# Three blocks of a first matmul by seven products instead of eight, with the instruction list made anew

## The chip, the cores and the metric

The kernel runs on one core of a Trainium2 chip. The metric is device time in microseconds, as the median of three runs. The engines are named as the profile names them: PE is TensorE, PEld its weight loads, DVE is VectorE, ACT is ScalarE, POOL is GpSimd, and SP is SyncE, whose queue issues most of the DMAs here.

## The reference

Retention (attention without a softmax, with a decay that depends on distance), followed by a dense two-layer network with a tanh-approximated GELU:

```python
# q, k, v: (8, 8, 576, 64)   batch, heads, positions, head_dim
gamma = 1.0 - 2.0 ** (-5.0 - np.arange(H))
Dmat = np.where(rel >= 0, gamma[:, None, None] ** rel, 0.0)      # rel = i - j
ret = (q @ k.transpose(0, 1, 3, 2)) / sqrt(64) * Dmat
x = (ret @ v).transpose(0, 2, 1, 3).reshape(4608, 512)           # tokens x d_model
h = x @ w_in                                                     # 512 -> 2048,  "mm1"
g = 0.5 * h * (1 + tanh(sqrt(2 / pi) * (h + 0.044715 * h**3)))
out = g @ w_out                                                  # 2048 -> 512,  "mm2"
```

## The kernel before

**The work.** The 4608 tokens are cut in two ways. Attention goes by *units*: 8 batches of 5 units (four of 128 positions and a tail of 64), numbered 0 to 39; eight of these are taken in pairs ("wide" units) at the start. The network goes by *blocks* of 512 tokens, numbered 0 to 8.

A unit's q, k and v are loaded into a slot of `pages` (7 slots of three pages, `raws[u % NR]`), cast to f16 with the decay factors (steps `q`, `k`, `v`), transposed (`D` by DMA, `t`/`y` by TensorE), and multiplied (step `B u,w`: scores and state sums of unit u, output of unit w). The masked scores (`m`), state sums (`a`, `o`) and f16 states (`z`) follow. Step `x` copies a unit's output, already transposed, into `xT`, a ring of 2048 tokens; mm1 reads its moving operand from there.

**mm1.** For a block, 2048 hidden features are made in 16 tiles of 128 features x 512 tokens. A step `N t,fc,part` takes two features' tiles for 256 of the tokens: 8 matmuls of 256 columns into one PSUM bank (line 708). A step `F` is the gelu of that bank on ScalarE, PSUM to the f16 tile `gT` (line 716). `M` and `G` are the same with other cuts (512 or 128 columns). The pool `ps_h` has two banks for this.

**mm2.** Blocks 1 to 7 and half of block 8 already go by a scheme of seven products: a pair of 128-token chunks, the two halves of the features and the two halves of the output columns form a 2 x 2 block product, and seven products of sums (`H`: sums of gT on VectorE into `ssum`; `T`: sums of w_out into `tsum`, made once) take the place of eight. A step `W t,pr,i` is one product (8 matmuls of 256 columns, line 809), a step `V t,pr,i` copies or adds a piece of the two banks of `ps_o` into the result tile `ost` (lines 241 and 768). The rest of mm2 are plain steps `O` (line 734) and `P` (line 857), and `S` and `Q` store.

**The order.** Nothing is scheduled by a framework. `ORDER` is a written list of some 1200 steps; the kernel walks through it and issues each step's instructions, so the list fixes the order on every engine and on every queue. Each engine works through its own instructions in that order; waits between engines follow from the tiles. A step that waits holds up whatever stands behind it on its engine or queue. `K` are filler matmuls near the start.

Of the kernel before, what the change touches and what calls it, by code (L numbers as in the profile page):

```python
# [10 lines left out]
AF = mybir.ActivationFunctionType  # L11
ALU = mybir.AluOpType
F32 = mybir.dt.float32
# [4 lines left out]
Z,1,v Z,2,g L,0,0 L,0,2 q,0 L,0,1 k,0,a L,2,0 v,0,g g I,2,g I,1,g K,4 K,2 t,0,q,o K,4 K,2 X,0 a,0,1  # L18
y,0,q,a q,2 I,0,g Z,3,v t,0,k,h y,0,k,v I,3,g z,0,1,a L,2,1 a,1,1 k,2,g K,4 K,4 K,2 t,2,k,h o,1,1
Y,0,1 L,4,1 I,5,g Z,4,g m,0,1 t,2,q,o k,4,a K,4 Y,0,0 y,2,k,a y,2,q,a z,1,1,v m,0,0 K,4 R,0 t,4,k,o  # L20
Y,2,1 I,4,g L,2,2 c Z,0,g x,1 x,0 K,3 N,0,0,0 m,2,1 L,4,0 N,0,2,0 I,7,g y,4,k,v v,2,g L,5,0 F,0,0,0
I,6,g N,0,6,0 F,0,6,0 F,0,2,0 Z,5,v L,5,1 X,2 q,4 Y,2,0 K,1 t,4,q,o N,0,4,0 N,0,10,0 a,2,1 z,2,1,v
m,2,0 k,5,g F,0,4,0 N,0,8,0 J,1,g y,4,q,v a,3,1 q,5 L,5,2 F,0,10,0 R,2 J,0,g B,4,-1 z,3,1,v t,5,q,o
# [26 lines left out]
H,2,0,2,v N,3,6,0 F,3,4,0 H,2,0,4,v S,1,1 H,2,1,1,v L,23,2 L,21,0 D,19 L,24,1 L,24,0 W,2,0,6  # L50
z,16,1,g V,2,0,2,a v,17,v B,17,16 a,17,0 V,2,0,1,v z,17,0,g a,17,1 N,3,2,0 S,1,2 x,16 m,17 F,3,6,0
W,2,0,7 z,17,1,v B,18,17 x,17 L,20,0 H,2,1,3,v W,2,0,5 L,22,1 L,25,0 F,3,2,0 V,2,0,3,v m,18 a,18,0
L,21,2 N,3,14,0 z,18,0,a a,18,1 W,2,0,4 V,2,0,4,v F,3,14,0 V,2,0,5,v N,3,8,1 q,21 L,22,0 W,2,0,3
k,21,v H,2,1,2,v W,2,1,1 V,2,1,0,a F,3,8,1 B,19,18 V,2,0,6,v j,0,a N,3,4,1 W,2,1,2 W,2,1,6 V,2,1,2,a
N,3,0,1 W,2,1,7 F,3,4,1 F,3,0,1 V,2,1,1,v S,1,3 V,2,1,3,v S,2,0 L,26,0 L,19,2 q,22 q,20 N,3,14,1
D,20 H,2,1,4,v F,3,14,1 v,20,g z,18,1,v x,18 L,22,2 W,2,1,4 N,3,6,1 W,2,1,5 V,2,1,5,v F,3,6,1
N,3,12,0 D,21 W,3,0,1 V,3,0,0,a L,25,1 F,3,12,0 N,3,10,1 m,19 v,19,v L,23,1 B,20,19 V,2,1,4,v a,20,0
L,23,0 k,22,g N,3,12,1 L,29,0 L,27,0 H,3,0,1,v H,3,0,2,v W,3,0,2 F,3,12,1 F,3,10,1 W,2,1,3 k,24,g
m,20 N,3,2,1 V,3,0,2,a V,2,1,6,v v,21,g x,19 a,20,1 z,20,0,g N,4,0,0 F,3,2,1 H,3,0,4,v v,22,g
B,21,20 k,23,a N,4,6,0 D,22 F,4,0,0 W,3,0,6 q,24 k,25,v F,4,6,0 N,4,4,0 H,3,0,3,v V,3,0,1,v N,4,12,0  # L60
F,4,4,0 a,21,0 x,20 a,21,1 H,3,1,1,v v,23,v z,20,1,a o,21,1 m,21 W,3,0,5 W,3,0,7 z,21,0,a D,24
V,3,0,3,v S,2,1 F,4,12,0 N,4,2,0 B,22,21 F,4,2,0 q,23 V,3,0,4,v H,3,1,2,v x,21 W,3,0,4 q,25
V,3,0,5,v L,26,1 a,22,0 W,3,0,3 S,2,2 L,27,2 m,22 N,4,12,1 W,3,1,1 z,22,0,a D,23 L,24,2 F,4,12,1
V,3,0,6,v q,27 N,4,2,1 j,5,v L,26,2 N,4,0,1 F,4,2,1 a,22,1 z,21,1,g z,22,1,a L,25,2 B,23,22 L,28,0
V,3,1,0,a N,4,14,0 W,3,1,2 F,4,0,1 H,3,1,3,v N,4,4,1 W,3,1,6 F,4,14,0 V,3,1,1,v i,4,v S,2,3 F,4,4,1
m,23 x,22 V,3,1,2,a M,4,8 G,4,8 W,3,1,5 v,24,g L,28,1 v,25,g M,4,10 a,23,0 q,26 v,26,v G,4,10 L,27,1
N,4,14,1 W,3,1,7 a,23,1 V,3,1,3,v F,4,14,1 L,31,2 z,23,1,g M,4,9 z,23,0,a L,29,1 k,27,a B,24,23
H,3,1,4,v N,4,6,1 D,25 G,4,9 k,26,a L,29,2 M,4,11 x,23 L,28,2 W,3,1,4 F,4,6,1 V,3,1,4,v V,3,1,5,v
D,26 m,24 W,3,1,3 N,5,0,0 G,4,11 i,5,g V,3,1,6,v B,25,24 q,28 F,5,0,0 L,30,2 S,3,0 H,4,0,1,v W,4,0,1
k,28,v H,4,0,2,v x,24 S,3,3 V,4,0,0,a a,25,0 z,25,0,v N,5,2,0 W,4,0,2 F,5,2,0 m,25 N,5,6,0 D,27 D,28  # L70
a,25,1 B,26,25 N,5,14,0 H,4,0,4,v v,28,g S,3,1 L,30,0 v,27,v F,5,6,0 V,4,0,2,a N,5,8,0 x,25 F,5,14,0
W,4,0,6 H,4,0,3,v F,5,8,0 a,26,0 a,26,1 V,4,0,1,v v,29,g z,25,1,g L,32,0 N,5,10,0 z,26,0,v W,4,0,7
L,31,1 N,5,4,0 V,4,0,3,v H,4,1,1,v W,4,0,4 m,26 F,5,10,0 H,4,1,2,v B,27,26 x,26 W,4,0,5 L,32,2
V,4,0,5,v F,5,4,0 N,5,10,1 o,26,1 N,5,4,1 q,29 F,5,10,1 V,4,0,4,v m,27 W,4,1,1 V,4,1,0,a L,30,1
N,5,12,0 S,3,2 a,27,0 L,35,0 W,4,0,3 q,30 H,4,1,3,v V,4,0,6,v k,30,v H,4,1,4,v F,5,12,0 W,4,1,2
j,7,g W,4,1,6 F,5,4,1 z,26,1,a N,5,6,1 z,27,0,g k,29,g a,27,1 N,5,14,1 V,4,1,2,a H,5,0,1,v L,31,0
q,31 V,4,1,1,v L,36,2 D,30 W,4,1,7 V,4,1,3,v k,31,a B,28,27 F,5,6,1 F,5,14,1 a,28,0 W,4,1,5 S,4,1
H,5,0,2,v N,5,12,1 a,28,1 D,29 V,4,1,4,v z,28,0,a x,27 v,31,g z,28,1,v z,27,1,g N,5,0,1 F,5,12,1
W,4,1,4 L,34,0 N,5,8,1 L,33,1 F,5,8,1 m,28 F,5,0,1 B,29,28 m,29 v,30,g i,7,a V,4,1,5,v W,4,1,3
N,5,2,1 x,28 B,30,29 L,34,1 F,5,2,1 H,5,0,4,v x,29 a,30,0 V,4,1,6,v W,5,0,1 m,30 H,5,0,3,v V,5,0,0,a  # L80
H,5,1,3,v v,32,v a,30,1 S,4,0 N,6,0,0 z,30,0,g L,33,0 W,5,0,2 q,33 W,5,0,6 V,5,0,2,a N,6,12,0
V,5,0,1,v W,5,0,7 D,31 B,31,30 F,6,0,0 k,34,a L,34,2 x,30 q,32 V,5,0,3,v H,5,1,1,v W,5,0,5 M,6,8
L,36,0 q,34 a,31,0 L,32,1 k,33,v L,33,2 F,6,12,0 W,5,0,4 H,5,1,2,v G,6,8 N,6,2,0 i,6,a m,31
V,5,0,5,v F,6,2,0 M,6,9 q,35 W,5,1,1 G,6,9 M,6,4 G,6,4 L,35,1 V,5,0,4,v L,38,1 N,6,2,1 S,4,2 S,5,1
z,30,1,g k,32,v L,39,2 F,6,2,1 D,32 W,5,0,3 M,6,5 a,31,1 V,5,1,0,a z,31,0,a j,4,a G,6,5 W,5,1,2
V,5,0,6,v M,6,11 B,32,31 v,33,g o,31,1 V,5,1,2,a W,5,1,7 M,6,6 G,6,11 S,5,0 S,4,3 a,32,0 G,6,6 x,31
z,32,0,a D,33 W,5,1,6 m,32 v,34,g V,5,1,1,v M,6,7 M,6,10 a,32,1 z,31,1,v j,1,a V,5,1,3,v z,32,1,a
B,33,32 L,37,1 a,33,0 W,5,1,4 L,36,1 G,6,7 N,6,0,1 k,36,a G,6,10 k,35,g z,33,0,a F,6,0,1 L,37,0
a,33,1 V,5,1,5,v L,35,2 v,35,g W,5,1,5 x,32 H,6,0,3,v m,33 N,6,12,1 D,34 D,35 H,5,1,4,v N,6,14,0
F,6,12,1 F,6,14,0 v,36,g B,34,33 q,36 V,5,1,4,v H,6,0,1,v N,6,14,1 W,6,0,1 W,5,1,3 k,38,a H,6,0,2,v  # L90
x,33 F,6,14,1 V,5,1,6,v V,6,0,0,a L,38,0 m,34 z,33,1,g N,7,0,0 F,7,0,0 B,35,34 L,38,2 q,38 W,6,0,2
V,6,0,2,a N,7,10,0 W,6,0,6 H,6,0,4,v H,6,1,1,v F,7,10,0 a,35,0 q,37 N,7,8,0 L,39,1 F,7,8,0 x,34 m,35
V,6,0,1,v z,35,0,a D,36 S,5,3 W,6,0,7 a,35,1 V,6,0,3,v z,35,1,g N,7,6,0 H,6,1,2,v W,6,0,4 k,37,g
N,7,2,0 D,37 B,36,35 V,6,0,5,v L,39,0 F,7,6,0 F,7,2,0 q,39 W,6,1,1 N,7,4,0 W,6,0,5 x,35 N,7,4,1
F,7,4,0 V,6,0,4,v L,37,2 W,6,0,3 N,7,0,1 F,7,4,1 S,5,2 i,3,a a,36,0 V,6,0,6,v a,36,1 N,7,2,1
V,6,1,0,a W,6,1,6 m,36 H,7,0,3,v v,38,v F,7,0,1 N,7,6,1 z,36,0,g V,6,1,1,v F,7,2,1 k,39,v W,6,1,2
N,7,12,0 F,7,6,1 V,6,1,2,a H,6,1,4,v D,39 v,37,g B,37,36 H,6,1,3,v W,6,1,5 W,6,1,7 x,36 N,7,14,0
o,36,1 z,36,1,a S,6,1 F,7,12,0 D,38 N,7,8,1 F,7,14,0 a,37,0 V,6,1,3,v V,6,1,4,v W,6,1,4 N,7,10,1
F,7,8,1 V,6,1,5,v W,7,0,1 a,37,1 m,37 W,6,1,3 z,37,0,v F,7,10,1 z,37,1,a S,6,0 N,7,12,1 B,38,37
i,2,g x,37 V,7,0,0,a F,7,12,1 j,2,v V,6,1,6,v H,7,0,1,v v,39,g N,7,14,1 F,7,14,1 H,7,0,2,v W,7,0,6  # L100
N,8,0,0 a,38,0 W,7,0,2 a,38,1 N,8,12,0 H,7,0,4,v F,8,0,0 m,38 H,7,1,1,v V,7,0,1,v S,6,3 N,8,2,0
z,38,0,v V,7,0,2,a W,7,0,7 S,6,2 F,8,2,0 F,8,12,0 W,7,0,5 B,39,38 V,7,0,3,v N,8,10,0 W,7,0,4 N,8,4,0
F,8,10,0 H,7,1,2,v V,7,0,4,v V,7,0,5,v x,38 W,7,1,1 W,7,0,3 V,7,1,0,a m,39 N,8,14,0 z,38,1,g B,-1,39
W,7,1,2 F,8,4,0 V,7,1,2,a N,8,6,0 V,7,0,6,v H,7,1,3,v F,8,14,0 W,7,1,6 N,8,8,0 W,7,1,7 H,7,1,4,v
x,39 F,8,6,0 V,7,1,1,v W,7,1,5 V,7,1,3,v W,7,1,4 F,8,8,0 N,8,10,1 N,8,14,1 V,7,1,5,v V,7,1,4,v
F,8,10,1 W,7,1,3 H,8,0,1,v W,8,0,1 V,8,0,0,a H,8,0,2,v N,8,0,1 S,7,3 F,8,14,1 F,8,0,1 V,7,1,6,v
S,7,2 W,8,0,6 V,8,0,1,v N,8,8,1 W,8,0,2 S,7,0 V,8,0,2,a S,7,1 H,8,0,3,v F,8,8,1 N,8,2,1 W,8,0,7
N,8,6,1 H,8,0,4,v W,8,0,5 F,8,2,1 V,8,0,3,v F,8,6,1 W,8,0,4 N,8,12,1 N,8,4,1 V,8,0,5,v O,8,8
V,8,0,4,v F,8,4,1 W,8,0,3 V,8,0,6,v F,8,12,1 O,8,9 O,8,10 O,8,11 S,8,0 P,0 P,1 E,0,v S,8,1 e,8,2,a
E,1,a S,8,2 Q,0 P,2 E,2,a Q,1 Q,2 w  # L110
# [4 lines left out]
def kernel(  # L115
# [23 lines left out]
    QF = 1.0 / math.sqrt(D)  # L139
    G = 64  # L140
    assert TAIL == G and D == 64 and H == 8 and NCT == HP

    const = ctx.enter_context(tc.tile_pool(name="const", bufs=1))
    sb = ctx.enter_context(tc.tile_pool(name="sb", bufs=3))
    ps_h = ctx.enter_context(tc.tile_pool(name="ps_h", bufs=2, space=bass.MemoryType.PSUM))
    ps_o = ctx.enter_context(tc.tile_pool(name="ps_o", bufs=2, space=bass.MemoryType.PSUM))
    ps_s = ctx.enter_context(tc.tile_pool(name="ps_s", bufs=1, space=bass.MemoryType.PSUM))
    ps_x = ctx.enter_context(tc.tile_pool(name="ps_x", bufs=1, space=bass.MemoryType.PSUM))
    ctx.enter_context(tc.manual_schedule())


# [793 lines left out]
```

## Time and profile before

| | us |
|---|---|
| median of 3 runs | 300.67 (300.24 to 301.27) |
| profiled execution | 301.17 |
| its span, first to last instruction | 299.1 |
| TensorE busy (4086 matmuls) | 286.2 |
| VectorE busy (408 instructions) | 185.2 |
| ScalarE busy (282 instructions) | 144.5 |
| GpSimd busy (125 instructions) | 80.7 |

The granted TensorE clock is 1.00 of full speed. A matmul's end is modelled and matmuls overlap, so the time of a row of matmuls is best read from start to start. In a row such as "L716 ACT ACTIVATE gT<-hps 128x512 f16<-128x512 f32 x144 | 84.8, 597 | 79.3 <-PE hps L708 79.0" stand the line, engine and operation, what is written from what, the shapes, the count, then busy time, mean nanoseconds of one, and the idle time of the engine ahead of it with what ended it. Most instructions of a kind share a line, since helpers (`copy_on`, `combine`) issue them.

### The profile page before, as it was taken

The numbers are of one execution on the slowest core, as the hardware profiler recorded it, in microseconds if no ns is written. First come the engines' busy times: TensorE is split into PE (matmuls) and PEld (weight loads), VectorE is DVE, ScalarE is ACT, GpSimd is POOL, SyncE is SP. The second block draws the span as 40 slices with busy tenths as digits, with TensorE's granted clock in tenths as the row PEclk, the third lists the DMA queues.
The fourth block names the chain that finished last, engine by engine and source line by source line (L and its number), as shares of the span: only waits on it lengthen the run. The fifth ranks groups of instructions, "written<-read, shape, count | busy, mean of one in ns | idle before, by whom it ended". The sixth has DMA issues, their size and how long they took to land.

```text
span 299.1 us, 9534 instructions
## 1 busy us (share of the span) xinstructions
PE 286.2 (96%) x4086; PEld 234.9 (79%) x4086; DVE 185.2 (62%) x408; ACT 144.5 (48%) x282; POOL 80.7 (27%) x125
## 2 busy tenths in 40 slices
PE   3898999999999999989999999999999999999995
PEld 1466777668887788878887888887788888888874
DVE  8566663599629687357835877777288274643310
ACT  2463663436346544335577445444584546433321
POOL 5980810391321312113121125134041130200000
PEclk9999999999999999999999999999999999999999
DMA  6999999937999987999997995897995507100303
GB/s 191 279 230 239 283 197 202 214 75 161 189 212 155 237 125 184 206 221 189 221 226 158 241 234 119 168 182 167 215 180 112 122 21 142 37 2 0 144 18 125
DMA packets 135370, 49.51 MB, mean 166 GB/s; under 512 B 117152, under 2 KB 129824, under 8 KB 135328
## 3 DMA queue, kind: packets, MB, share of 16 engines
q1 hardware_dynamic: 130976, 44.71, 67.8%
q0 software_dynamic: 4352, 4.20, 8.4%
q8 instruction: 32, 0.52, 0.8%
q14 instruction: 10, 0.08, 0.1%
HBM read 36.70 MB, written 9.44 MB: 154 GB/s over the span
## 4 chain that ended last, share of the span: by engine, by line
PE 79%; DMA 6%; POOL 6%; DVE 4%; SPq 2%; issue 1%; ACT 1%; ACTq 0%; POOLq 0%; DVEq 0%
PE hps L708 37%; PE ops L809 27%; PE ops L734 6%; DMA w_in_sb<-in_moe_w_in_dram 3%; PE sk L516 2%; PE x L498 2%; POOL w_in_sb L212 2%; DMA pages<-in_q_dram 2%; DMA pages<-in_v_dram 2%; PE sk L526 1%; POOL wide L407 1%; PE x L536 1%; SPq L189 1%; PE ops L857 1%; POOL v L392 1%
## 5 line engine op out<-in xcount | busy, mean ns | idle before, releaser
L708 PE MATMUL hps<-xT,w_in_sb 128*128 128x256 f16 (+2 forms) x1120 | 143.4, 276 | 1.5 <-DMA w_in_sb<-in_moe_w_in_dram 1.5
L716 ACT ACTIVATE gT<-hps 128x512 f16<-128x512 f32 x144 | 84.8, 597 | 79.3 <-PE hps L708 79.0
L708 PEld LDWEIGHTS <-w_in_sb 128*128 128x128 f16 x1120 | 105.4, 98 | 20.7 <-DMA w_in_sb<-in_moe_w_in_dram 2.5
L809 PEld LDWEIGHTS <-ssum 128*128 128x128 f16 x480 | 46.1, 98 | 7.4 <-issue 0.6
L809 PE MATMUL ops<-tsum,ssum 128*128 128x256 f16 x360 | 46.1, 273 | 0.0
L809 PEld LDWEIGHTS <-gT 128*128 128x128 f16 x360 | 34.6, 98 | 6.8 <-issue 1.5
L392 POOL TENSOR_TENSOR v<-pages,dec 128x512 f16<-128x512 f32 (+1 forms) x24 | 23.8, 1001 | 51.9 <-DMA pages<-in_v_dram 38.0
L768 DVE TENSOR_TENSOR ost<-u,ops 128x256 f32<-128x256 f32 x45 | 18.5, 417 | 27.0 <-PE ops L809 25.4
L809 PE MATMUL ops<-w_out_sb,gT 128*128 128x256 f16 x240 | 31.2, 273 | 1.4 <-DVE ost L768 1.4
L768 DVE TENSOR_TENSOR u<-u,ops 128x256 f32<-128x256 f32 x30 | 12.5, 418 | 29.6 <-PE ops L809 19.9
L243 POOL CAST sz<-s 64x256 f16<-64x256 f32 x26 | 14.7, 564 | 55.4 <-DVE s L667 37.9
L392 DVE TENSOR_TENSOR qk<-pages,dec 128x512 f16<-128x512 f32 (+1 forms) x32 | 22.1, 696 | 10.0 <-DMA pages<-in_q_dram 10.0
L768 DVE TENSOR_TENSOR ssum<-gT,ssum 128x1024 f16<-128x1024 f16 x30 | 22.7, 758 | 0.2
L768 DVE TENSOR_TENSOR ssum<-gT 128x1024 f16<-128x1024 f16 x30 | 21.8, 732 | 0.8 <-ACT gT L716 0.8
L555 ACT ACTIVATE xT<-x 128x512 f16<-128x512 f32 (+1 forms) x26 | 14.4, 563 | 13.8 <-PE x L536 13.7
L651 DVE TENSOR_TENSOR ret<-sk,mask 128x512 f16<-128x512 f32 (+1 forms) x32 | 19.8, 618 | 1.4 <-PE sk L526 1.4
L734 PE MATMUL ops<-w_out_sb,gT 128*128 128x512 f16 x80 | 19.6, 379 | 0.0
L241 ACT CAST sz<-s 64x256 f16<-64x256 f32 x36 | 14.5, 402 | 8.8 <-DVE s L667 6.8
L685 POOL TENSOR_TENSOR sz<-s,gend 64x256 f16<-64x256 f32 x8 | 7.7, 959 | 36.9 <-DVE s L667 22.6
L667 DVE TENSOR_TENSOR s<-s,sk 128x256 f32<-128x256 f32 x36 | 15.0, 416 | 4.2 <-PE sk L526 3.6
L241 ACT COPY ost<-ops 128x256 f32<-128x256 f32 (+2 forms) x20 | 7.9, 394 | 18.0 <-PE ops L809 9.9
L809 PE MATMUL ops<-w_out_sb,ssum 128*128 128x256 f16 x120 | 15.6, 273 | 0.5 <-DVE ost L768 0.5
(96 smaller groups left out, 273.5 us busy)
## 6 DMA issues: line engine op xcount, KB each, us to landing
out_dram<-ost SPq DMA_DIRECT2D x35, 256.0 KB, 3.2
pages<-in_q_dram SPq DMA_DIRECT2D x32, 256.0 KB, 5.0
pages<-in_k_dram SPq DMA_DIRECT2D x24, 256.0 KB, 4.8
pages<-in_v_dram SPq DMA_DIRECT2D x24, 256.0 KB, 4.4
pages<-in_v_dram SPq DMA_DIRECT2D x4, 512.0 KB, 7.5
pages<-in_k_dram SPq DMA_DIRECT2D x4, 512.0 KB, 6.9
w_in_sb<-in_moe_w_in_dram POOLq DMA_DIRECT2D x8, 256.0 KB, 10.0
w_out_sb<-in_moe_w_out_dram POOLq DMA_DIRECT2D x8, 256.0 KB, 10.6
```

The source lines that it names most:

```text
L241: nc.scalar.copy(out=o, in_=i)
L243: (nc.vector if eng == "v" else nc.gpsimd).tensor_copy(out=o, in_=i)
L392: eng.tensor_tensor(out=out, in0=s["raw"][:, i, 0:n], in1=dec[:, i // 2, s["j"], 0:n].unsqueeze(2).to_broadcast([128, n, D]), op=ALU.mult,)
L555: nc.scalar.activation(out=xT[:, :, o : o + G * (b - a)].rearrange("c p (h s) -> c p h s", s=G), in_=x[:, a:b].rearrange("c h p s -> c p h ...
L651: nc.vector.tensor_tensor(out=ret[:, :, 0:n], in0=now["sk"][:, :, 0, 0:n], in1=mask.unsqueeze(1).unsqueeze(1).to_broadcast([128, 2, n, G]) ...
L667: nc.vector.tensor_tensor(out=s32, in0=state[0], in1=kv, op=ALU.add)
L685: (nc.vector if eng == "v" else nc.gpsimd).tensor_tensor(out=z[o : o + 64, :, hl, :], in0=s32[o : o + 64], in1=gend[o : o + 64], op=ALU.mult,)
L708: nc.tensor.matmul(hps[:, i, :], w_in_sb[:, ct, 128 * (fc + i) : 128 * (fc + i) + 128], xT[:, ct, TB * t % XR + lo : TB * t % XR + hi], st ...
L716: nc.scalar.activation(out=gTs[t][:, fc : fc + TB // (hi - lo), lo:hi], in_=h.pop((t, fc, lo)), func=AF.Gelu_apprx_tanh, bias=0.0, scale=1.0,)
L734: nc.tensor.matmul(ops[t, tcc], gTs[t][:, ft, 128 * tcc : 128 * tcc + 128], w_out_sb[:, ft, :], start=(ft == 0), stop=(ft == NFC - 1),)
L768: (nc.vector if eng == "v" else nc.gpsimd).tensor_tensor(out=out, in0=a, in1=b, op=op)
L809: nc.tensor.matmul(p["ps", bank][:, HN * col : HN * col + HN], a[:, k], b[:, k], start=(k == 0 and i in (1, 6)), stop=(k == HK - 1), skip_ ...
```

## The change

mm1 of blocks 6, 7 and 8 is done by seven products too. A block is cut into 4 groups of four features' tiles (512 features). In a group, the two halves of the features (256 each), the two halves of d_model (256 each) and the two halves of the tokens (256 each) form a 2 x 2 block product. A step `A t,g,i` is one product: 4 matmuls of 256 columns. Products 1, 6, 7 and 4 are summed up in the first bank, 2, then 5 and 3 in the second. A step `l t,g,i,eng` takes a part out: parts 0 to 2 copy the first bank into `hu0` to `hu2`, parts 3 to 5 add the second bank to one of them. A step `f t,g,i` is a gelu of 128 x 512; the first reads the bank, the other three read the sums in SBUF.

The sums of x (`s t,i`, four for a block) and of w_in (`U i,part`, eight in all) are made on VectorE. They, and the parts' sums, lie in the pages of load slots 3 to 6. So from unit 31 on only slots 0 to 2 are loaded. The ring `xT` is 1536 tokens long. The masked scores of the wide units, which lay in the ring's end, get a slot of their own. The PSUM pools of mm1 and mm2 become one tile each, whose two banks are taken in turn. The list is the same up to `N,3,...` apart from filler steps, and new from there on.

```diff
 ORDER = """
...
-B,33,32 L,37,1 a,33,0 W,5,1,4 L,36,1 G,6,7 N,6,0,1 k,36,a G,6,10 k,35,g z,33,0,a F,6,0,1 L,37,0
...
+N,5,0,1 a,31,0 F,5,12,1 z,30,1,g x,30 H,5,0,2,v L,34,1 a,31,1 z,31,0,a F,5,0,1 W,4,1,3 A,6,0,1 s,6,1
+L,32,2 V,4,1,5,v s,6,2 l,6,0,0,a W,5,0,1 v,32,g k,34,g D,32 A,6,0,6 l,6,0,1,a A,6,0,2 m,31 H,5,0,3,v
+B,32,31 L,35,0 V,5,0,0,a s,6,3 V,4,1,6,v A,6,0,7 W,5,0,6 s,6,4 q,34 l,6,0,2,a l,6,0,3,v x,31 L,33,2
...
+    LATE = 31
+    def raw_of(u):
+        return u % NR if u < LATE else (u - LATE) % 3
...
-    XR = 4 * TB
+    XR = 3 * TB
...
+    banks = {
+        "h": ps_h.tile([128, 2, 512], F32, name="banks_h"),
+        "o": ps_o.tile([128, 2, 512], F32, name="banks_o"),
+    }
+    turn = {"h": 0, "o": 0}
+    def take(pool):
+        turn[pool] += 1
+        return banks[pool][:, turn[pool] % 2]
...
     def wide_ret():
-        return xT[:, :, XR - 512 : XR].rearrange("c p (l j s) -> c p l j s", l=2, j=2)
+        if "wide" not in st:
+            st["wide"] = slot([128, HP, 2, 2, 128], F16, "ret_wide")
+        return st["wide"]
...
+    sums = pages[:, 9:21].rearrange("p n h d -> p (n h d)").bitcast(F16)
+    wsum = sums[:, 0:8192].rearrange("p (i c g f) -> p i c g f", i=4, c=2, g=4)
+    xsum = sums[:, 8192:10240].rearrange("p (i c s) -> p i c s", i=4, c=2)
+    csum = pages[:, 19:21].rearrange("p n h d -> p n (h d)").rearrange("p n (i s) -> n p i s", i=2)
...
+    def sum_w(i, part):
...
+        x, y = ((a(1, 0), a(1, 1)), (a(0, 0), s[0]), (a(1, 0), a(0, 0)), (a(0, 1), s[1]))[i - 1]
+        combine("v", s[i - 1], x, y, ALU.subtract)
...
+    def sum_x(t, i):
+        b, s = [[blk_x(t, y, x) for x in range(2)] for y in range(2)], [xsum[:, n] for n in range(4)]
+        x, y = ((b[0][1], b[0][0]), (b[1][1], s[0]), (b[1][1], b[0][1]), (b[1][0], s[1]))[i - 1]
+        combine("v", s[i - 1], x, y, ALU.add if i in (2, 3) else ALU.subtract)
...
+    def product_h(t, g, i):
...
+        if i in (1, 2):
+            p["ps", i - 1] = take("h").rearrange("c (i n) -> c i n", i=2)
...
+        w, x, bank = {
+            1: (a(0, 0), blk_x(t, 0, 0), 0), 2: (a(0, 1), blk_x(t, 1, 0), 1),
+            3: (wsum[:, 3, :, g], blk_x(t, 1, 1), 1), 4: (a(1, 1), xsum[:, 3], 0),
+            5: (wsum[:, 0, :, g], xsum[:, 0], 1), 6: (wsum[:, 1, :, g], xsum[:, 1], 0),
+            7: (wsum[:, 2, :, g], xsum[:, 2], 0),
+        }[i]
+        for n in range(2):
+            for c in range(2):
+                nc.tensor.matmul(
+                    p["ps", bank][:, n], w[:, c, 128 * n : 128 * n + 128], x[:, c],
+                    start=(n == 0 and c == 0 and i in (1, 2, 5)), stop=(c == 1),
+                    skip_group_check=True,
+                )
+    def part_h(t, g, i, eng):
+        p = groups[t, g]
+        if i < 3:
+            p["u", i] = sb.tile([128, 2, 256], F32, tag=f"hu{i}", name=f"hu{i}", bufs=1)
+            copy_on(eng, p["u", i], p["ps", 0])
+            return
+        turn["c"] += 1
+        p["c", i - 2] = csum[turn["c"] % 2]
+        combine(eng, p["c", i - 2], p["u", (0, 2, 1)[i - 3]], p["ps", 1], ALU.add)
+    def gelu_h(t, g, i):
+        p = groups[t, g]
+        f, o = 4 * g + (2 if i in (0, 2) else 0), 256 if i in (2, 3) else 0
+        nc.scalar.activation(
+            out=gTs[t][:, f : f + 2, o : o + 256], in_=p["ps", 0] if i == 0 else p["c", i],
+            func=AF.Gelu_apprx_tanh, bias=0.0, scale=1.0,
+        )
...
```

## The prediction

> **What bounds the kernel now.** I read the page first (busy shares, slices), then the chain that ended last, then busy time by stage, then who TensorE waited for, then the timeline around those waits.
>
> ```profile
> span 299.1 us, 9534 instructions
> PE 286.2 (96%) x4086; PEld 234.9 (79%) x4086; DVE 185.2 (62%) x408; ACT 144.5 (48%) x282; POOL 80.7 (27%) x125
> PE   3898999999999999989999999999999999999995
> PE 79%; DMA 6%; POOL 6%; DVE 4%; SPq 2%; issue 1%; ACT 1%; ACTq 0%; POOLq 0%; DVEq 0%
> ```
>
> TensorE is the bound: 96% busy, full in every slice behind the first, and four fifths of the chain. The 6% of DMA and 6% of POOL in the chain lie before 31 us, where w_in's pieces arrive. The stages of blocks 6, 7 and 8 (from each block's first mm1 step to the next one's) are about these windows (PE, PEld, DVE, ACT, POOL busy, clock, DMA):
>
> ```profile
> 194.00:225.00 31.00, 31.00 (x472) 24.61 (x460) 21.38 (x43) 18.70 (x39) 9.68 (x11) 1.00 0.95 188
> 225.00:258.00 33.00, 32.53 (x479) 28.95 (x477) 20.71 (x44) 16.09 (x34) 5.62 (x10) 1.00 0.42 94
> 258.00:290.00 32.00, 32.00 (x325) 28.13 (x323) 11.25 (x26) 11.42 (x23) 0.96 (x1) 1.00 0.09 34
> ```
>
> TensorE has no hole there, VectorE is busy for 53.3 of 96 us, ScalarE for 46.2. So mm1's matmuls in these stages lie on the path, one for one, and VectorE and ScalarE have room. What a matmul costs, and how fast a neighbour answers, is in the timeline:
>
> ```profile
> 280.19 1.04 PE L708 MATMUL hps<-xT,w_in_sb 128*128 128x256 f16 x8
> 281.06 1.04 PE L809 MATMUL ops<-w_out_sb,gT 128*128 128x256 f16 x8
> 283.69 1.04 PE L708 MATMUL hps<-xT,w_in_sb 128*128 128x256 f16 x8
> 284.76 0.60 ACT L716 ACTIVATE gT<-hps 128x512 f16<-128x512 f32 x1 [1.15 <-PE hps L708]
> ```
>
> Eight matmuls of 256 columns take 0.87 us start to start, 0.109 each. ScalarE starts 1.07 us behind the first of the eight, so 0.20 us behind their share of TensorE.
>
> **What goes.** An mm1 block is 128 matmuls of 256 columns; by seven products it is 4 groups x 7 products x 4 matmuls = 112. The instruction stream of the changed kernel has 336 of them for blocks 6 to 8 where 384 stood (some as half as many of 512 columns, at the same rate). 48 x 0.109 = **5.24 us** off the path. A filler step of one matmul at 24.4 us goes as well; w_in's arrival at 26.45 us hides that: 0.
>
> **What comes.** Per group: six part steps (copies out of a PSUM bank, or adds of a kept part and a bank; 72 in all) and four gelus, as many as before; per block four sums of x; once, eight sums of w_in. Nothing of it is on TensorE. Their rows, the nearest in shape:
>
> ```profile
> L243 DVE COPY ost<-ops 128x512 f32<-128x512 f32 x2 | 1.4, 692 | 3.3 <-PE ops L734 3.2
> L241 ACT COPY ost<-ops 128x512 f32<-128x512 f32 x3 | 1.8, 586 | 3.5 <-PE ops L734 3.5
> L651 DVE TENSOR_TENSOR ret<-sk,mask 128x512 f16<-128x512 f32 x24 | 16.4, 684 | 0.4 <-PE sk L526 0.4
> 106.64 0.69 DVE L392 TENSOR_TENSOR v<-pages,dec 128x512 f16<-128x512 f32 x1
> 107.24 0.42 DVE L675 TENSOR_TENSOR old<-s,gseg 128x256 f32<-128x256 f32 x1
> 107.58 0.68 DVE L392 TENSOR_TENSOR qk<-pages,dec 128x512 f16<-128x512 f32 x1
> ```
>
> The last three rows give the pitch: in a full queue the next VectorE operation starts 0.60 us behind one of 0.69, and 0.34 behind one of 0.42. Gelus in a row start 0.51 apart, ScalarE's copies 0.50. Summing every step of the new list by pitch (in brackets by duration), as TensorE / VectorE / ScalarE: block 6's stage 30.7 / 25.0 (29.8) / 16.9; block 7's 28.6 / 26.0 (30.5) / 17.7; block 8's 30.6 / 22.1 (25.9) / 14.3. Of before, by duration, VectorE has 19.3, 18.8 and 14.8: 52.9 where the windows above show 53.3, so the method holds. Block 7's 26.0 are 13 part steps (7.8), 8 mm2 sums of 0.64 (5.1), 12 assembling steps (4.1), 6 sums of x taken as 0.34 (half of 1024 f16 elements; 2.0), and attention (7.0). So VectorE goes from half full to 82%, 91% and 72% by pitch, and hides under TensorE with little left. The eight sums of w_in (8 x 0.64) fall in block 5's stage, 26.1 of 34.7 us: 0, as long as that cover holds; without it 5.1.
>
> **The links.** A group has only the two banks of mm1's pool. Product 1 fills the first, a copy empties it, product 6 is added on top, again a copy, then 7, a copy, 4, a gelu; the other bank has 2, 5 and 3 with an add behind each. Each is a link: TensorE is in order, so what is queued behind a product that waits (mm2 products, attention) waits too. A link needs 0.20 + the operation + 0.06 (the resume in the stall below: 131.94 + 0.42 to 132.42): 0.86 with ScalarE, 0.95 with VectorE. Counting the TensorE work that the list puts between the ends of each link, of 82 links 12 have exactly one mm2 product or its like (0.87, no margin), one has 0.44, 17 of VectorE's have 1.31 (0.35 over), the rest more. So the order fills them, but tightly. A group takes at least 4 x (0.44 + 0.86) = 5.2 us in its first bank, against 7.2 to 7.7 us of TensorE work per group: no bound by itself. What a late queue does is here:
>
> ```profile
> 128.35 1.04 POOL L392 TENSOR_TENSOR v<-pages,dec 128x512 f16<-128x512 f32 x1 [1.68 <-DMA pages<-in_v_dram]
> 129.01 1.53 DVE L392 TENSOR_TENSOR qk<-pages,dec 128x512 f16<-128x512 f32 x2 [1.81 <-DMA pages<-in_q_dram]
> 131.94 0.42 DVE L768 TENSOR_TENSOR ost<-u,ops 128x256 f32<-128x256 f32 x1
> 132.42 1.03 PE L809 MATMUL ops<-w_out_sb,gT 128*128 128x256 f16 x8 [1.37 <-DVE ost L768]
> ```
>
> A late load held VectorE's queue, and TensorE stood 1.37 us. With 0.5 more that is all TensorE waited after 100 us.
>
> Price of the links: ScalarE is busy for 0.55 of the stages, so a copy with no margin meets on average half of a gelu's 0.51 there: 13 x 0.14 = 1.8. VectorE's lateness, 0.85 x 0.30 on average, stays inside 0.35, except behind operations that POOL has stretched:
>
> ```profile
> 189.27 1.04 POOL L392 TENSOR_TENSOR v<-pages,dec 128x512 f16<-128x512 f32 x1 [1.91 <-issue]
> 189.35 1.51 DVE L768 TENSOR_TENSOR ssum<-gT,ssum 128x1024 f16<-128x1024 f16 x1
> ```
>
> The 0.68 became 1.51. About one mm2 sum in five is stretched; of 26 in the stages that is five, each up to 0.8 late, 0.45 over the margin, and a third of them in front of a tight link: 0.8. At most all five count: 1.8 + 5 x 0.45 = 4.1. The new list may also place the 1.8 us of old waits better: I take -1.0. Net **+1.6**, from -1.8 to 4.1 at the ends. The section "SBUF: two separate sides" of the Trainium skill's page "SBUF — State Buffer" says that a VectorE operation with two SBUF inputs and a GpSimd operation that reads SBUF exclude each other for their whole length. By it the new adds, with one input in PSUM, are never stretched, and only the sums are; the trace agrees so far (adds onto PSUM never took over 0.423 us); were the adds stretched as often, the term would double.
>
> **What else moves.** Merged bank tiles: the same waits on readers, fewer on TensorE itself: 0. The masked scores of the wide units in a slot of their own: same operation, same place: 0. The one-element Gelu that moves from the end into block 5's stage: 0.2 of ScalarE's time, 0. Behind the last gelu the same mm2 steps, copies and stores stand in another order: 0. Some casts move to POOL (15.8 us of it in the three stages by the old list, 21.1 by the new): that is in the stretching above. The x ring of 1536 tokens: each unit writes over tokens whose mm1 is a stage back in the list: 0. From unit 31 on loads have three slots where they had seven: a load waits until the unit three back is cast, and on SP's queue the transposes and stores behind it wait too. Loads land in about 5 us and a stage has four or five units, so a load issued when its slot is free has 10 us and more: 0, at worst one 1.37 us stall for a late one.
>
> **Sum.** Profiled execution 301.17 (span 299.1 and 2.07 around it) - 5.24 + 1.6 = 297.5. The median shown is 300.67, 0.5 lower: **297.0**.
>
> **Rivals.** *Clean*: no link costs anything and old waits go: 300.67 - 5.24 - 1.0 = 294.4. For: TensorE stood only 1.8 us in 200 under the old list. Against: margins of nothing in 12 links.
> *The links lose more than the products save* (slower): every tight link meets one more operation in its queue: 13 x 0.51 + 17 x 0.25 = 10.9; three quarters of it give 300.67 - 5.24 + 8.2 = 303.6. It decides from 5.2 us on, about half of the tight links. For: VectorE has never been at 91% here. Against: the trace shows in-order queues kept to within 0.5 us nearly everywhere.
> *VectorE sets the pace*: operations follow end to end, not by pitch. Then block 7 needs 30.5 and about 1.8 of stretch against 28.6, block 6 29.8 + 1.8 against 30.7: 4.6 us, 300.0. Against: the starts 0.60 apart. The section "The DRAIN you can't avoid" in the skill's page "VectorE: DVE Perf Modes" (Trainium skill) says that the next operation starts only when the pipe has emptied, which would give this case; the rows at 106.64 to 107.58 show starts 0.09 ahead of the ends.
> *Late loads*: three stalls like that at 131 us, 4.1, on top of 1.6: 301.1.
> That the change takes no work off is out, since the stream has 48 matmuls fewer.
>
> **Chances.** Forecast (295.2 to 299.5) 0.60, clean 0.10, links 0.18, VectorE 0.08, loads 0.04. A difference under 0.3% (0.9 us) can't be told from none here. Faster 0.70, same 0.12 (VectorE, loads), slower 0.18. From 294.0 to 301.5 lie the forecast, most of clean, VectorE and loads: 0.80.
>
> **What would show it.** Right: about 48 fewer matmuls' time on TensorE (busy near 281), VectorE near 227 us by duration, TensorE's waits on part steps 1 to 4 us, none over 0.6. Wrong: TensorE idle of over 5 us behind 190 us, ended by ScalarE's or VectorE's part steps (links), VectorE without a gap in block 7 (pace), or waits on loads of units 31 to 39.

## The result and the profile after

The changed kernel takes **389.46 us** (median of 4 runs, 387.33 to 391.9) where the kernel before takes 300.46 (4 runs): a ratio of 1.298 (1.286 to 1.309). The prediction of 297.0 us (294.0 to 301.5) was 92 us too low, and its sign was wrong. The profiled execution took 387.43. One execution further below, of the kernel with four bank tiles, took 1003.68 us where its other three took 297 to 299; it is left out of that kernel's ratio, and the median of the other three is 299.02.

First the page of the changed kernel, in the order in which the page of before was read: span, busy time of each engine, TensorE in 40 slices, the chain.

```profile
span 385.7 us, 9674 instructions
PE 300.9 (78%) x4085; PEld 238.0 (62%) x4085; DVE 222.4 (58%) x473; ACT 153.1 (40%) x296; POOL 81.1 (21%) x137
PE   5787869987889889877688788767776778677775
PE 65%; ACT 16%; DVE 14%; issue 5%; DVEq 0%; POOL 0%; ACTq 0%; POOLq 0%
```

No engine is the bound any more. TensorE was 96% busy and is 78% busy: it stands for 84.8 us (385.7 - 300.9) where it stood for 12.9. VectorE and ScalarE did not fill up; they have come into the chain with 14% and 16% all the same, which is how taking turns looks on a page: each engine in the chain, none of them full. And the loss is not in the last three blocks, where the products are new. The slices are thin from the second on, although the two lists are the same up to the first step of block 3 but for fillers. The trace gives the start of each block's first mm1 matmul (us):

| start of | block 0 | block 1 | block 2 | block 3 | block 6 | step `O,8,8` behind block 8 | span |
|---|---|---|---|---|---|---|---|
| before | 20.29 | 44.05 | 75.22 | 105.83 | 197.32 | 288.05 | 299.1 |
| after | 21.76 | 49.27 | 92.3 | 129.01 | 245.1 | 373.29 | 385.7 |

23.2 us are gone by block 3, before a single product, sum or late load of the change has been issued. Next, whom TensorE waited for in the changed kernel (engine and line that waited, who released it, us in total, times, longest):

```profile
PE banks_h L747 <- ACT gT L755: 23.9, 36, 1.7
PE banks_h L938 <- DVE pages L807: 12.7, 15, 1.9
PE banks_h L938 <- ACT hu L260: 6.8, 10, 0.9
PE banks_o L850 <- DVE ost L807: 6.5, 8, 1.2
PE banks_h L938 <- ACT gT L957: 5.1, 6, 1.9
```

The longest row is not the new products' (L938) but that of the old steps `N` (L747), which wait for the gelu (L755) 36 times. Before, no such row stood: the only wait of TensorE on a reader of a bank was 1.8 us on `ost`. The timeline of the changed kernel in block 2 shows what kind of wait it is (start, duration, engine, line, operation, in brackets the idle time ahead and who ended it):

```profile
109.25 1.03 PE L747 MATMUL banks_h<-xT,w_in_sb 128*128 128x256 f16 x8 [0.25 <-ACT gT L755]
110.32 0.60 ACT L755 ACTIVATE gT<-banks_h 128x512 f16<-128x512 f32 x1 [1.12 <-PE banks_h L747]
110.96 1.03 PE L747 MATMUL banks_h<-xT,w_in_sb 128*128 128x256 f16 x8 [0.68 <-ACT gT L755]
112.03 0.60 ACT L755 ACTIVATE gT<-banks_h 128x512 f16<-128x512 f32 x1 [1.12 <-PE banks_h L747]
```

TensorE fills a bank, ScalarE empties it, and only then is the *other* bank begun, though it has been free all the time. The pool has two banks and works as if it had one. The brackets name ScalarE's gelu as what ended the wait, and the profile infers that from semaphore events: what holds TensorE is a wait that stands in the program. Eight matmuls start every 1.71 us: 0.87 of matmuls, 0.20 until the gelu starts, 0.60 of gelu, 0.04 until TensorE resumes.

Readers are held as well. At the start of block 0 in the same timeline, two steps `N` fill both banks, 16 matmuls on end, since nothing has yet been read:

```profile
21.76 1.91 PE L747 MATMUL banks_h<-xT,w_in_sb 128*128 128x256 f16 x16
23.70 0.60 ACT L755 ACTIVATE gT<-banks_h 128x512 f16<-128x512 f32 x1 [0.69 <-PE banks_h L747]
```

The gelu of the first bank could start 1.07 us behind the first matmul (0.87 + 0.20); it starts 1.94 behind it, when the second bank is full too. The suspect is an edit that the prediction put at nothing: the two banks of a pool are now slices of one tile.

### The profile page after: what moved, and what is told of

It is laid out like the page before. It is cut to its first block, busy times and chain, and to the rows that moved or that the text cites. A ratio compares the mean times of both kernels' runs of the same rounds, so it can differ in the third digit from the quotient of the medians.

```text
span 385.7 us, 9674 instructions
## 1 busy us (share of the span) xinstructions
PE 300.9 (78%) x4085; PEld 238.0 (62%) x4085; DVE 222.4 (58%) x473; ACT 153.1 (40%) x296; POOL 81.1 (21%) x137
## 3 DMA queue, kind: packets, MB, share of 16 engines
q1 hardware_dynamic: 130976, 44.71, 53.3%
## 4 chain that ended last, share of the span: by engine, by line
PE 65%; ACT 16%; DVE 14%; issue 5%; DVEq 0%; POOL 0%; ACTq 0%; POOLq 0%
PE banks_h L747 23%; PE banks_o L850 20%; PE banks_h L938 9%; ACT gT L755 8%; PE banks_o L773 4%; DVE pages L807 4%; PE banks_h L985 3%; ACT hu L260 2%; DVE ost L807 2%; ACT gT L957 2%; ACT ost L260 1%; PE sk L550 1%; ACT sz L260 1%; PE x L528 1%; DVE u L807 1%
## 5 line engine op out<-in xcount | busy, mean ns | idle before, releaser
L747 PE MATMUL banks_h<-xT,w_in_sb 128*128 128x256 f16 (+2 forms) x784 | 100.7, 277 | 26.1 <-ACT gT L755 23.9
L747 PEld LDWEIGHTS <-w_in_sb 128*128 128x128 f16 x784 | 74.9, 100 | 44.8 <-issue 32.3
L755 ACT ACTIVATE gT<-banks_h 128x512 f16<-128x512 f32 x96 | 55.1, 597 | 100.4 <-PE banks_h L747 100.4
L850 PE MATMUL banks_o<-tsum,ssum 128*128 128x256 f16 x360 | 46.0, 272 | 7.5 <-ACT ost L260 4.1
L807 DVE TENSOR_TENSOR ost<-u,banks_o 128x256 f32<-128x256 f32 x45 | 18.5, 418 | 41.8 <-PE banks_o L850 29.5
L807 DVE TENSOR_TENSOR pages<-hu,banks_h 128x512 f32<-128x512 f32 x36 | 24.7, 686 | 28.0 <-PE banks_h L938 13.7
L850 PE MATMUL banks_o<-w_out_sb,gT 128*128 128x256 f16 x240 | 31.1, 272 | 2.1 <-DVE ost L807 1.0
L938 PE MATMUL banks_h<-pages 128*128 128x256 f16 x144 | 20.7, 271 | 12.2 <-DVE pages L807 8.3
L938 PEld LDWEIGHTS <-pages 128*128 128x128 f16 x192 | 18.5, 97 | 18.5 <-issue 15.9
L938 PEld LDWEIGHTS <-w_in_sb 128*128 128x128 f16 x144 | 13.8, 97 | 18.2 <-issue 16.6
L938 PE MATMUL banks_h<-xT,w_in_sb 128*128 128x256 f16 x96 | 14.4, 271 | 13.2 <-ACT gT L957 5.1
L957 ACT ACTIVATE gT<-pages 128x512 f16<-128x512 f32 x36 | 22.0, 629 | 4.6 <-DVE pages L807 4.5
L773 PE MATMUL banks_o<-w_out_sb,gT 128*128 128x512 f16 x80 | 20.6, 392 | 1.7 <-DVE ost L807 1.0
```

The costliest lines, as they stand in the source:

```text
L747: nc.tensor.matmul(hps[:, i, :], w_in_sb[:, ct, 128 * (fc + i) : 128 * (fc + i) + 128], xT[:, ct, TB * t % XR + lo : TB * t % XR + hi], st ...
L755: nc.scalar.activation(out=gTs[t][:, fc : fc + TB // (hi - lo), lo:hi], in_=h.pop((t, fc, lo)), func=AF.Gelu_apprx_tanh, bias=0.0, scale=1.0,)
L773: nc.tensor.matmul(ops[t, tcc], gTs[t][:, ft, 128 * tcc : 128 * tcc + 128], w_out_sb[:, ft, :], start=(ft == 0), stop=(ft == NFC - 1),)
L807: (nc.vector if eng == "v" else nc.gpsimd).tensor_tensor(out=out, in0=a, in1=b, op=op)
L850: nc.tensor.matmul(p["ps", bank][:, HN * col : HN * col + HN], a[:, k], b[:, k], start=(k == 0 and i in (1, 6)), stop=(k == HK - 1), skip_ ...
L938: nc.tensor.matmul(p["ps", bank][:, n], w[:, c, 128 * n : 128 * n + 128], x[:, c], start=(n == 0 and c == 0 and i in (1, 2, 5)), stop=(c = ...
```

## The experiments

**Four tiles in place of two.** The changed kernel, all else as it is; each bank is a tile of its own, again taken in turn.

```diff
-        "h": ps_h.tile([128, 2, 512], F32, name="banks_h"),
-        "o": ps_o.tile([128, 2, 512], F32, name="banks_o"),
+        "h": [ps_h.tile([128, 512], F32, name=f"bank_h{i}") for i in range(2)],
+        "o": [ps_o.tile([128, 512], F32, name=f"bank_o{i}") for i in range(2)],
...
-        return banks[pool][:, turn[pool] % 2]
+        return banks[pool][turn[pool] % 2][:, :]
```

> The changed kernel with each PSUM bank of mm1's and mm2's pools a tile of its own (four one-bank tiles, taken in turn as before); list, products, load slots and ring as in the changed kernel. Theory 'one tile' (a tile of two banks is held as one: a reader waits for the newest write to either bank, a write for the readers of either): the loss goes, and the forecast of 297 us is to be seen, 293 to 303. Rival 'links' (the seven products' chain of copies loses it) and rival 'list' (the new list is slower by itself): only the 23 us go that were lost where the lists are the same, so 355 to 370.

Measured: 299.2 us; ratio to before 0.990 (0.986 to 0.994). The whole loss is gone, though the new list, the products, the shorter ring and the wide units' own slot are all still in this kernel. Its page:

```profile
span 297.7 us, 9703 instructions
PE 281.2 (94%) x4085; PEld 234.6 (79%) x4085; DVE 221.0 (74%) x473; ACT 154.0 (52%) x296; POOL 84.8 (28%) x137
PE   3798999999999999969999999999999999999995
```

The same 4085 matmuls, the same VectorE, ScalarE and GpSimd counts; TensorE stands for 16.5 us instead of 84.8. The rest of the 88.0 us between the spans is TensorE's busy time, 300.9 against 281.2: a run of eight matmuls with a gap behind it counts as 1.03 and not 0.87, and the granted clock of the changed kernel was 0.985, of this one 1.00. In its timeline, at the same two steps as in the rows of block 2 above (`N,2,4,1` and `N,2,0,1`), TensorE runs on through both banks, 28 matmuls on end, and the gelu of the first bank starts while the second is being filled:

```profile
90.33 3.65 PE L748 MATMUL bank_h<-xT,w_in_sb 128*128 128x256 f16 x28
91.40 0.60 ACT L756 ACTIVATE gT<-bank_h 128x512 f16<-128x512 f32 x1 [0.71 <-PE bank_h L748]
92.28 0.60 ACT L756 ACTIVATE gT<-bank_h 128x512 f16<-128x512 f32 x1 [0.28 <-PE bank_h L748]
```

**The one edit on the kernel before.** The kernel before with its list, ring and steps, and only its rotating one-bank tiles made slices of one tile per pool.

```diff
-    ps_h = ctx.enter_context(tc.tile_pool(name="ps_h", bufs=2, space=bass.MemoryType.PSUM))
+    ps_h = ctx.enter_context(tc.tile_pool(name="ps_h", bufs=1, space=bass.MemoryType.PSUM))
...
+        "h": ps_h.tile([128, 2, 512], F32, name="banks_h"),
...
-        h[t, fc, lo] = hps = ps_h.tile([128, TB // n, n], F32, tag="h", name="hps")
+        h[t, fc, lo] = hps = take("h").rearrange("c (i n) -> c i n", n=n)
...
```

> The kernel before, with its own list, eight products in mm1, seven load slots and the long ring, where only the two banks of mm1's pool become one tile, and the two of mm2's. Theory 'one tile': slower from the first mm1 tiles on. The changed kernel lost 23.2 us by the time that the lists part (105.8 us before, 129.0 after); at that rate over the whole kernel 300 becomes 345 to 375. Rivals 'links' and 'list': 299 to 303, since neither is in it.

Measured: 354.59 us, ratio 1.176 (1.173 to 1.180). It reaches block 3 at 129.17 us, the changed kernel at 129.01, the kernel before at 105.83. The page of this run and the largest of TensorE's waits in it:

```profile
PE 296.9 (85%) x4086; PEld 236.4 (67%) x4086; DVE 186.1 (53%) x408; ACT 142.9 (41%) x282; POOL 79.1 (23%) x125
PE banks_h L717 <- ACT gT L725: 28.5, 44, 1.7
```

So the merged tile is enough for a loss without anything else of the change, and its mark is the same: step `N` waits for the gelu, at most 1.7 us. The loss is smaller here (53 us, against 90 between the changed kernel and its split form) and the kernel before has no L938: the new products' waits, 24.6 us in the changed kernel's rows above, are missing in it.

**One pool at a time.** The changed kernel with only mm1's banks split, and with only mm2's.

```diff
 # after_split_h: mm1's pool alone
-        "h": ps_h.tile([128, 2, 512], F32, name="banks_h"),
+        "h": [ps_h.tile([128, 512], F32, name=f"bank_h{i}") for i in range(2)],
         "o": ps_o.tile([128, 2, 512], F32, name="banks_o"),
 # after_split_o: mm2's pool alone
         "h": ps_h.tile([128, 2, 512], F32, name="banks_h"),
-        "o": ps_o.tile([128, 2, 512], F32, name="banks_o"),
+        "o": [ps_o.tile([128, 512], F32, name=f"bank_o{i}") for i in range(2)],
```

> The changed kernel with mm1's two banks as tiles of their own and mm2's two banks still one tile. Theory 'one tile': TensorE's waits at mm1 lines (26 us at line 747 and 25 at line 938 in the changed kernel's profile) go, those at mm2's (12 us) stay or grow: 305 to 325. Rivals: 350 to 370.

> The changed kernel with mm2's two banks as tiles of their own and mm1's two banks still one tile. Theory 'one tile': the 12 us of waits at mm2's lines go, the 51 at mm1's stay: 340 to 380. Rivals: 350 to 380, so this run tells little by itself; it is to share the loss out between the two pools.

Measured: with mm2's banks still merged 324.85 us (ratio 1.078, 1.072 to 1.085), with mm1's still merged 369.13 (1.225, 1.221 to 1.229). Against 299.2 with both split that is 26 us for mm2's pool, 70 for mm1's, and 90 for both: less than the sum of 96, which fits stalls that partly cover each other. mm2's banks come in pairs too (a product in each, `V` reading both), and the list puts mm1's matmuls between its products, which probably covers most of what is held there. TensorE's largest wait in the kernel with mm2's banks merged (four tiles leave 0.8 us of it):

```profile
PE banks_o L851 <- DVE ost L808: 7.9, 12, 1.5
```

**The way of cutting.** Is it the form of the slice, an index on a middle dimension? Here the tile is flat, and a bank is 512 of its 1024 columns.

```diff
-        "h": ps_h.tile([128, 2, 512], F32, name="banks_h"),
+        "h": ps_h.tile([128, 1024], F32, name="banks_h"),
...
-        return banks[pool][:, turn[pool] % 2]
+        return banks[pool][:, 512 * i : 512 * i + 512]
```

> The changed kernel with each pool's two banks still one tile, but as 1024 columns of which a bank is the slice of 512, where it was the middle index of a tile of 2 x 512. Theory 'one tile', as it stands (a PSUM tile over two banks is held as one, however it is cut): no change, 384 to 393. Rival 'cut' (only the index into the middle dimension hides which bank is meant): 297 to 301, as with tiles of one bank.

Measured: 389.73 us, ratio 1.294 (1.288 to 1.299): the changed kernel to within its spread. It is one tile in two banks that costs, however it is cut.

**Rotating tiles.** The changed kernel with pools as before: two buffers each, a new one-bank tile at each use.

```diff
-    ps_h = ctx.enter_context(tc.tile_pool(name="ps_h", bufs=1, space=bass.MemoryType.PSUM))
+    ps_h = ctx.enter_context(tc.tile_pool(name="ps_h", bufs=2, space=bass.MemoryType.PSUM))
...
-        return banks[pool][:, turn[pool] % 2]
+        return (ps_h if pool == "h" else ps_o).tile([128, 512], F32, tag=pool, name=f"bank_{pool}")[:, :]
```

> The changed kernel with the pools as in the kernel before: every use takes a new one-bank tile of a rotating pool of two, for mm1 and for mm2. Theory 'one tile': the same as with four fixed one-bank tiles (299.2 there), 297 to 301. Rival 'fixed tiles' (the gain of the split kernel comes of fixed tiles, not of one bank each): over 305.

Measured: 299.21 us, ratio 0.992 (0.989 to 0.995). No difference from four fixed tiles can be told. What matters is one tile for each bank, not whether it is new at each use; a reason to give up the pools can't be found in the time.

**Two attempts at the rest.** With the tiles split the kernel is 0.8 to 1.0% faster than before, where the prediction wanted 1.2%. Two edits on the list of the split kernel try places where it lost: the fillers near the start as before, and on top of that one load of unit 26 moved behind a later one, away from a stall at 128 us.

```diff
 # split_k: the split kernel, fillers as before (K 6, 6, 10 where 9, 6, 7 stood)
-... g I,2,g I,1,g K,4 K,4 K,1 t,0,q,o K,4 K,2 X,0 ... k,2,g K,4 K,3 t,2,k,h ...
+... g I,2,g I,1,g K,4 K,2 t,0,q,o K,4 K,2 X,0 ... k,2,g K,4 K,4 K,2 t,2,k,h ...
 # split_k_load: this, and
-L,26,0 L,24,0 H,2,1,2,v ... q,24 L,25,1 F,3,14,1 ...
+L,24,0 H,2,1,2,v ... q,24 L,25,1 L,26,0 F,3,14,1 ...
```

> The kernel with four one-bank tiles, its filler steps at the start as in the kernel before (6, 6, 10 matmuls where the changed list has 9, 6, 7); total the same. In the split kernel's trace TensorE waited 1.2 us for a copy at 13.9 us, and the first mm1 tile started at 20.78 us where it was 20.29 before. If the fillers did that: the first mm1 tile at 20.3, and 0 to 0.6 us at the end, since w_in's arrival at 26.5 us bounds this part in both. Otherwise no change: 299 within 1.

> As split_k, and the load of unit 26's q, which the new list puts ahead of unit 24's q and 22 us ahead of its cast, put behind unit 25's k instead. In the split kernel VectorE waited 6.3 us for a load of q (122 to 128 us) and TensorE lost 3.1 us behind it, against 1.5 us in that stage of the kernel before. If that load stood in the way: 1 to 3 us faster than split_k. If the queue was full anyway: no change, 299 within 1.

Measured: 298.36 (0.992, 0.989 to 0.995) and 299.52 (0.994, 0.991 to 0.996). Neither can be told from the split kernel or from the other. With the fillers as before, the first mm1 matmul started at 21.01 us, not at 20.3; with rotating tiles and the changed list's fillers it had been 20.28. So the fillers are not what sets it. The move of the load changed little of what it was made for; VectorE waited 6.31 us for that q page in the split kernel (first row), 6.02 in `split_k`, and 5.92 with the load moved as well (second row):

```profile
128.13 0.87 DVE L424 TENSOR_TENSOR qk<-pages,dec 128x512 f16<-128x512 f32 x1 [6.31 <-DMA pages<-in_q_dram]
```
```profile
126.33 1.52 DVE L424 TENSOR_TENSOR qk<-pages,dec 128x512 f16<-128x512 f32 x1 [5.92 <-DMA pages<-in_q_dram]
```

The split kernel's DMA engines were 98% busy from 112 to 126 us (85% before), so several transfers crowd there, and the order of one may not be the matter. That was not taken further.

## Why the prediction was wrong, and where it was right

**The step that failed** is one sentence under "What else moves": "Merged bank tiles: the same waits on readers, fewer on TensorE itself: 0." It was argued from the names, not from rows: the products name the same banks in the same turn, so I took the waits to stay. Its price, changed kernel against split kernel, is 389.46 - 299.2 = **+90 us**. Two banks in one tile are held as one: a write waits for the readers of either bank, a reader for the newest write to either. The kernel before held no merged PSUM tile, so no row of it could show this. But its numbers could have bounded it: a link was priced at 0.86 us (0.20 + gelu + 0.06), and 0.87 of matmuls + 0.86 is 1.73 for a bank that is not doubled, against 1.71 measured. For 144 gelus the end of the range on the bad side would have been 144 x 0.86 = 124 us. A zero without a named cover was the mistake. None of the rivals named the bank tiles either.

**The mark of the wrong rival came true.** The text said that TensorE idle of over 5 us behind 190 us, ended by part steps, would show that the links lose more than the products save. The changed kernel has just that (12.7 + 6.8 us on L938 ended by part steps, and 5.1 more ended by gelus). Yet with split tiles and the same links those waits are nearly gone. The split kernel's waits of TensorE from 199 to 290 us, all of them:

```profile
PE bank_h L939 <- DVE pages L808: 0.7, 1, 0.7
PE bank_o L851 <- DVE ost L808: 0.3, 1, 0.3
```

So the *links* rival falls, though its mark appeared; the 23 us lost ahead of block 3 already spoke against it.

**The rest of the sum, read on the split kernel**, which is the changed kernel less that one step:

- *Products, -5.24.* TensorE is busy for 281.2 us, 5.0 less than before; the text said near 281. Right.
- *Links, net +1.6.* Its parts were 1.8 for ScalarE, 0.8 for stretched sums, -1.0 for old waits placed better. TensorE's idle time by stretch (the stretch less TensorE's busy time in it) is 0.47 us before and 1.13 split between block 6's first mm1 matmul and `O,8,8`: +0.66 where 2.6 stood. The two stretches (before, then split; the second column is the length, the third TensorE's busy time):

```profile
197.32:288.05 90.73, 90.26 (x1178) 77.49 (x1176) 51.23 (x106) 42.99 (x88) 16.00 (x20) 1.00 0.47 104
199.40:287.40 88.00, 86.87 (x1126) 76.75 (x1124) 77.61 (x152) 55.08 (x108) 17.57 (x26) 1.00 0.48 108
```

The tight links were nearly free: TensorE waited once for a part step, 0.7 us, where 1 to 4 us was named (the 0.7 is above the 0.6 that none should pass); the 0.3 in the fence above is an assembling step of mm2. The credit of 1.0 for old waits did not come: between blocks 3 and 6 idle time went from 1.37 to 2.63 (most of it the stall at 128 us), ahead of block 3 from 8.06 to 9.58. The sum: 0.66 + 1.26 + 1.52 + 0.13 (behind `O,8,8`) = +3.6, and -5.0 + 3.6 = -1.4, which is the difference of the spans (297.7 - 299.1). By the ratios it is -1.9 to -4.2 for the split kernel, with the forecast's -3.6 inside. What adds the 1.5 us of idle time ahead of block 3 is open: with the fillers restored it is 9.4, against 9.6.
- *VectorE hides under TensorE.* Busy 221.0 us, forecast 227; in the three stages it is busy for 96, 94 and 75%, where 82, 91 and 72% were forecast. Busy time counts an overlap of two operations once, and a sum of durations counts it twice; the prediction's test of its method (52.9 against 53.3) set the one against the other, and the durations in those windows of before add up to 59.5. In the split kernel they add up to 31.8, 28.9 and 25.2 us by stage, where 29.8, 30.5 and 25.9 were forecast. The split kernel's windows at the tightest place (stretch, length, then busy time of PE, PEld, DVE, ACT, POOL):

```profile
220.00:240.00 20.00, 19.45 (x310) 17.29 (x310) 19.55 (x40) 13.42 (x26) 8.89 (x12) 1.00 0.69 152
```

VectorE is busy for 98% of it and TensorE for 97%; TensorE idles for 0.55 us. Three rows of VectorE there (split kernel's timeline) show why a sum of durations misleads:

```profile
229.38 0.68 DVE L808 TENSOR_TENSOR pages<-hu,bank_h 128x512 f32<-128x512 f32 x1
229.98 0.69 DVE L808 TENSOR_TENSOR ssum<-gT 128x1024 f16<-128x1024 f16 x1
230.58 0.62 DVE L808 TENSOR_TENSOR pages<-xT 128x512 f16<-128x512 f16 x1
```

The starts are 0.60 apart, each ahead of the end before it, as in the rows of before. Block 6's stage took 29.6 us and block 7's 27.3: end to end the 31.8 and 28.9 us of operations would not fit in them, and the *VectorE sets the pace* rival falls. The section that the prediction named for that rival, "The DRAIN you can't avoid" in the Trainium skill's "VectorE: DVE Perf Modes", goes on to say that a next operation that is not held back starts earlier, which the prediction left out. These starts, 0.08 and 0.09 us ahead of the ends, agree with that.

- *Stretching by GpSimd.* The 36 new adds onto PSUM from 199 to 290 us took 0.673 to 0.689 us, none stretched, though nine of them ran beside a GpSimd instruction for 0.2 us or more; four of the 26 sums of `ssum`, with SBUF inputs alone, took 0.88 to 1.20 (0.68 in the median), each beside one. The prediction had five. That is what the Trainium skill's "SBUF — State Buffer", section "SBUF: two separate sides", led one to expect, and the trace agrees.
- *Late loads.* No wait of TensorE behind 199 us ends on a load: three slots are enough here.

## What to carry to other kernels

Keep one PSUM tile for each bank that is to be double buffered; two banks cut from one tile worked as one buffer here, which cost 30% in the changed kernel and 18% in the kernel before. When an edit rewrites how a buffer is declared, price the wait that it may add with the rows at hand (producer + answer + reader + resume for each use) before it is put at nothing. When a loss starts ahead of the place where the large part of a change begins, look for the small edits that apply everywhere.

## What the runs showed that I had not expected

- A PSUM tile over two banks is held whole: 389.5 us against 299.2 with a tile for each bank, 354.6 against 301.1 in the kernel before, and alike for a tile cut by a middle dimension or by columns (389.5, 389.7). The scratch pages in SBUF, which are one tile too and hold load slots, sums of x and parts' sums at once, showed no such waits between their pages: in the split kernel most of VectorE's writes into them ran while another engine was reading another part. What makes the difference between the two was not tried.
- A small part of the loss is clock. In the changed kernel TensorE's granted clock was 0.84 between 40 and 60 us and 0.92 between 180 and 200, where the split kernel had 1.00; that is some 5 us of the 90 (estimated as 0.16 x 20 + 0.08 x 20). Gaps behind the matmuls are not enough to bring it about: from 245 to 373 us the changed kernel's TensorE idled for 27% of the time and the clock was 1.00, and the kernel before with merged tiles kept 1.00 from 20 to 340 us, with gaps throughout. Behind the stall at 128 us the clock was 0.91 (120 to 140 us) with rotating tiles and with the load moved, and 1.00 in the split kernel. What decides it is open.
